# Gradients of a gated MLP: two hidden blocks per round, untransposed weight gradients, and half-filled matmuls placed side by side

## The chip, the cores and the metric

The kernel runs on one core of a Trainium2 chip. The metric is the device time of one execution in microseconds (us), as the median over several executions. Its engines are TensorE (PE; PEld is its weight load), VectorE (DVE), ScalarE (ACT), GpSimd (POOL) and SyncE (SP, which here only issues DMA). Matmuls write into PSUM, which has eight banks of 512 float32 values on each of 128 partitions; everything else lies in SBUF.

## The reference

The reference is a forward pass and its gradients. A layer normalisation with a learned shift and scale goes through a spectral filter (a 2-D FFT, a product, an inverse FFT), and a second one through a gated MLP without a nonlinearity:

```python
def _B_ref(x, w_gate, w_up, w_down):      # x: 1 x 2048 x 576, F = 4608
    g = jnp.einsum('bsd,df->bsf', x, w_gate)
    u = jnp.einsum('bsd,df->bsf', x, w_up)
    h = g * u
    return jnp.einsum('bsf,fd->bsd', h, w_down)

h = _layernorm(x) * (1 + ca) + sa
x = x + ga * _A_ref(h, A_w_r, A_w_i)
h = _layernorm(x) * (1 + cb) + sb
x = x + gb * _B_ref(h, B_w_gate, B_w_up, B_w_down)
```

The outputs are x and the gradients of eight inputs, in bfloat16. The change concerns the gated MLP alone. With 2048 tokens, 576 model dimensions and 4608 hidden units it needs, for each block of 128 hidden units:

- g and u (the projections), recomputed, and from them h = g u, gg = gh u and gu = gh g, where gh is the gradient of h (computed in an earlier stage and read back from DRAM);
- the gradients of the three weights: h^T times the incoming gradient (576 columns), and gg and gu against the normalised input;
- the contribution to the gradient of the input: gg times w_gate^T plus gu times w_up^T, summed over all 36 blocks.

576 is four and a half times 128, so wherever the model dimension lies on the partitions, a fifth piece has only 64 rows.

## The kernel before

The stage ahead of the loop computes gh for all blocks and stores it. Its staging tile `ghh_st` comes from a pool of two buffers:

```python
u4w = hs.enter_context(tc.tile_pool(name="u4w", bufs=2))
...
for j in range(nfb):
    fb = fb0 + j
    st = u4w.tile([128, NT, 128], BF, name="ghh_st")
    for sb4 in range(4):
        pt = u4ps.tile([128, 4, 128], FP32, name="u4p")
        for m in range(5):
            nc.tensor.matmul(pt[:], lhsT=wdT[:, m, j * 128:(j + 1) * 128], rhs=goT[:, 4 * sb4:4 * sb4 + 4, m, :], start=(m == 0), stop=(m == 4))
        evac(st[:, 4 * sb4:4 * sb4 + 4, :], pt[:])       # ScalarE and VectorE in turn
    nc.sync.dma_start(ghhT_d[fb * 128:(fb + 1) * 128, :], st[:].rearrange("f t p -> f (t p)"))
```

The normalised input is held twice: `h2p` with tokens on the partitions, padded from 576 to 640 columns (DP) with zeros, and `h2T`, its transpose, made by one DMA.

The loop over the 36 blocks (NFB; NT is 16 tiles of 128 tokens):

```python
gups  = tile_pool(name="gups",  bufs=3, space=PSUM)
u8ps  = tile_pool(name="u8ps",  bufs=3, space=PSUM)
u57ps = tile_pool(name="u57ps", bufs=2, space=PSUM)

def emit_u57(fb_, sfs_):                      # the three weight gradients of one block
    for ti_, (sf, rhs_n) in enumerate(((sfs_[0], gon), (sfs_[1], h2n), (sfs_[2], h2n))):
        so = stg.tile([128, DP], BF, name="so")
        for h in range(2):
            pw = u57ps.tile([128, 512], FP32, name="u57p")
            for t in range(NT):
                nc.tensor.matmul(pw[:, 0:288], lhsT=sf[:, t, :], rhs=rhs_n[:, t, h * 288:(h + 1) * 288], start=(t == 0), stop=(t == NT - 1))
            nc.scalar.copy(so[:, h * 288:(h + 1) * 288], pw[:, 0:288])
        if ti_ == 0:
            nc.sync.dma_start(out_6[...], so[:, 0:D])
        else:                                 # gate and up: to be stored transposed
            ptr = u57ps.tile([128, 5, 128], BF, name="u57p")
            for m in range(5):
                nc.tensor.transpose(ptr[0:KD[m], m, :], so[:, m * 128:m * 128 + KD[m]], ident[:])
            # ... two ScalarE copies to woT, two stores

for fb in range(NFB):
    # ... every 2nd block: load wgu, its fifth piece zeroed to 128 rows; every 4th: wT by ten DMA transposes
    for sb4 in range(4):
        ts_ = slice(4 * sb4, 4 * sb4 + 4)
        for wi_, dstT in enumerate((gT, uT)):             # the projections
            pt = gups.tile([128, 4, 128], FP32, name="gup")
            for m in range(5):
                nc.tensor.matmul(pt[:], lhsT=wgu[:, wi_, m, jw * 128:(jw + 1) * 128], rhs=h2T[:, ts_, m, :], start=(m == 0), stop=(m == 4))
            nc.scalar.copy(dstT[:, ts_, :], pt[:])
        # ... hhT = gT * uT, ggT = ghh * uT, guT = ghh * gT on VectorE
    # ... hh_sf, gg_sf, gu_sf: DMA transposes of hhT, ggT, guT; a store of hhT
    if pend:
        emit_u57(*pend.pop(0))                            # of the block before
    for t in range(NT):                                   # the gradient of the input
        for h in range(2):
            pu = u8ps.tile([128, 512], FP32, name="u8p")
            nc.tensor.matmul(pu[:, 0:288], lhsT=ggT[:, t, :], rhs=wT[:, 0, jt, h * 288:(h + 1) * 288], start=True, stop=False)
            nc.tensor.matmul(pu[:, 0:288], lhsT=guT[:, t, :], rhs=wT[:, 1, jt, h * 288:(h + 1) * 288], start=False, stop=True)
            # ... acc += pu on VectorE (a copy for the first block)
    pend.append((fb, sfs))
```

A scheduler orders the instructions of each engine, so what is written one after the other here may be mixed on the engine: before the change, the projections of a block are mixed with the input gradient of another.

Of the kernel before, what the change touches and what calls it, by code (L numbers as in the profile page):

```python
# [9 lines left out]
FP32 = mybir.dt.float32  # L10
# [9 lines left out]
NT = 16  # L20
S = 2048
D = 576
# [58 lines left out]
def build(ctx, tc, A_x, A_w_r, A_w_i, B_w_gate, B_w_up, B_w_down, c_in, w_mod, grad_out,  # L81
# [256 lines left out]
    with ExitStack() as hs:  # L338
# [62 lines left out]
        for fb0 in range(0, NFB, FB4):  # L401
# [11 lines left out]
                evac(wdT[0:64, 4, j * 128:(j + 1) * 128], ptw[0:64, 4, :])  # L413
            for j in range(nfb):
                fb = fb0 + j
                st = u4w.tile([128, NT, 128], BF, name="ghh_st")
                for sb4 in range(4):
                    pt = u4ps.tile([128, 4, 128], FP32, name="u4p")
                    for m in range(5):
                        nc.tensor.matmul(pt[:], lhsT=wdT[:, m, j * 128:(j + 1) * 128], rhs=goT[:, 4 * sb4:4 * sb4 + 4, m, :], start=(m == 0), stop=(m == 4))  # L420
                    evac(st[:, 4 * sb4:4 * sb4 + 4, :], pt[:])
                nc.sync.dma_start(ghhT_d[fb * 128:(fb + 1) * 128, :], st[:].rearrange("f t p -> f (t p)"))
# [6 lines left out]
    with ExitStack() as ms:  # L429
# [8 lines left out]
        with ExitStack() as ls:  # L438
# [5 lines left out]
            nc.vector.tensor_copy(mb2h[:], mb2[:, 0:2 * D])  # L444
            nc.gpsimd.dma_start(gon[:], go_v)
            nc.vector.tensor_tensor(out=gon[:], in0=gon[:], in1=gb_b.unsqueeze(1).to_broadcast([128, NT, D]), op=MUL)
            nc.gpsimd.memset(h2p[:, :, D:DP], 0.0)
            for c4 in range(4):
                x1c = lp2.tile([128, 4, D], FP32, name="x1c")
                nc.sync.dma_start(x1c[:], x1_d[:, 4 * c4:4 * c4 + 4, :])  # L450
# [1 line left out]
                for tt in range(4):  # L452
                    t = 4 * c4 + tt
                    n = lp2.tile([128, D], FP32, name="ln2n")
                    nc.scalar.activation(out=n[:], in_=x1c[:, tt, :], func=ACT.Identity, bias=nmr2[:, tt:tt + 1], scale=rstd2[:, tt:tt + 1])
                    nc.vector.tensor_tensor(out=n[:], in0=n[:], in1=opcb_b, op=MUL)
                    nc.vector.tensor_tensor(out=h2p[:, t, 0:D], in0=n[:], in1=sb_b, op=ADD)
            nc.sync.dma_start_transpose(out=h2T[:].rearrange("q t m p -> q (t m) p"), in_=h2p[:].rearrange("p t d -> p (t d)"))
        with ExitStack() as bs:
            FBW = 2  # L460
            FBT = 4
            wp = bs.enter_context(tc.tile_pool(name="wp", bufs=2))
            wtp = bs.enter_context(tc.tile_pool(name="wtp", bufs=2))
            ghp = bs.enter_context(tc.tile_pool(name="ghp", bufs=2))
            tp = bs.enter_context(tc.tile_pool(name="tp", bufs=2))
            tp2 = bs.enter_context(tc.tile_pool(name="tp2", bufs=2))
            sfp = bs.enter_context(tc.tile_pool(name="sfp", bufs=2))
            stg = bs.enter_context(tc.tile_pool(name="stg", bufs=4))
            wot = bs.enter_context(tc.tile_pool(name="wot", bufs=3))
            gups = bs.enter_context(tc.tile_pool(name="gups", bufs=3, space=PSUM))  # L470
            u8ps = bs.enter_context(tc.tile_pool(name="u8ps", bufs=3, space=PSUM))
            u57ps = bs.enter_context(tc.tile_pool(name="u57ps", bufs=2, space=PSUM))
            pend = []

            def emit_u57(fb_, sfs_):
                for ti_, (sf, rhs_n) in enumerate(((sfs_[0], gon), (sfs_[1], h2n), (sfs_[2], h2n))):
                    so = stg.tile([128, DP], BF, name="so")
                    for h in range(2):
                        pw = u57ps.tile([128, 512], FP32, name="u57p")
                        for t in range(NT):  # L480
                            nc.tensor.matmul(pw[:, 0:288], lhsT=sf[:, t, :], rhs=rhs_n[:, t, h * 288:(h + 1) * 288], start=(t == 0), stop=(t == NT - 1))  # L481
                        nc.scalar.copy(so[:, h * 288:(h + 1) * 288], pw[:, 0:288])  # L482
                    if ti_ == 0:
                        nc.sync.dma_start(out_6[fb_ * 128:(fb_ + 1) * 128, :], so[:, 0:D])
                    else:
                        ptr = u57ps.tile([128, 5, 128], BF, name="u57p")
                        for m in range(5):
                            K = KD[m]
                            nc.tensor.transpose(ptr[0:K, m, :], so[:, m * 128:m * 128 + K], ident[:])
                        woT = wot.tile([128, 5, 128], BF, name="woT")  # L490
                        nc.scalar.copy(woT[:, 0:4, :], ptr[:, 0:4, :])
                        nc.scalar.copy(woT[0:64, 4, :], ptr[0:64, 4, :])
                        odst = out_4 if ti_ == 1 else out_5
                        nc.sync.dma_start(odst[0:512, fb_ * 128:(fb_ + 1) * 128].rearrange("(m q) f -> q m f", q=128), woT[:, 0:4, :])
                        nc.sync.dma_start(odst[512:576, fb_ * 128:(fb_ + 1) * 128], woT[0:64, 4, :])
            wgu = None
            wT = None
            for fb in range(NFB):
                if fb % FBW == 0:
                    nb = min(FBW, NFB - fb)  # L500
                    wgu = wp.tile([128, 2, 5, FBW * 128], BF, name="wgu")
                    nc.gpsimd.memset(wgu[64:128, :, 4, :], 0.0)
                    for wi_, wsrc in enumerate((B_w_gate, B_w_up)):
                        eng = nc.sync if wi_ == 0 else nc.gpsimd
                        eng.dma_start(wgu[:, wi_, 0:4, 0:nb * 128], wsrc[0:512, fb * 128:(fb + nb) * 128].rearrange("(m q) f -> q m f", q=128))
                        eng.dma_start(wgu[0:64, wi_, 4, 0:nb * 128], wsrc[512:576, fb * 128:(fb + nb) * 128])
                if fb % FBT == 0:
                    nb = min(FBT, NFB - fb)
                    wT = wtp.tile([128, 2, FBT, D], BF, name="wT")
                    for wi_, wsrc in enumerate((B_w_gate, B_w_up)):  # L510
                        for m in range(5):
                            K = KD[m]
                            nc.sync.dma_start_transpose(out=wT[:, wi_, 0:nb, m * 128:m * 128 + K], in_=wsrc[m * 128:m * 128 + K, fb * 128:(fb + nb) * 128])
                jw = fb % FBW
                jt = fb % FBT
                ghh = ghp.tile([128, NT, 128], BF, name="ghh")
                nc.gpsimd.dma_start(ghh[:].rearrange("f t p -> f (t p)"), ghhT_d[fb * 128:(fb + 1) * 128, :])
                gT = tp2.tile([128, NT, 128], BF, name="gT")
                uT = tp2.tile([128, NT, 128], BF, name="uT")
                hhT = tp.tile([128, NT, 128], BF, name="hhT")  # L520
                ggT = tp.tile([128, NT, 128], BF, name="ggT")
                guT = tp.tile([128, NT, 128], BF, name="guT")
                for sb4 in range(4):
                    ts_ = slice(4 * sb4, 4 * sb4 + 4)
                    for wi_, dstT in enumerate((gT, uT)):
                        pt = gups.tile([128, 4, 128], FP32, name="gup")
                        for m in range(5):
                            nc.tensor.matmul(pt[:], lhsT=wgu[:, wi_, m, jw * 128:(jw + 1) * 128], rhs=h2T[:, ts_, m, :], start=(m == 0), stop=(m == 4))  # L528
                        nc.scalar.copy(dstT[:, ts_, :], pt[:])  # L529
                    nc.vector.tensor_tensor(out=hhT[:, ts_, :], in0=gT[:, ts_, :], in1=uT[:, ts_, :], op=MUL)  # L530
                    nc.vector.tensor_tensor(out=ggT[:, ts_, :], in0=ghh[:, ts_, :], in1=uT[:, ts_, :], op=MUL)
                    nc.vector.tensor_tensor(out=guT[:, ts_, :], in0=ghh[:, ts_, :], in1=gT[:, ts_, :], op=MUL)
                nc.gpsimd.dma_start(hhT_d[:, :, fb, :].rearrange("tp f x -> f tp x"), hhT[:].rearrange("f (tp ti) p -> f tp (ti p)", ti=2))  # L533
                sfs = []
                for nm, srcT in (("hh_sf", hhT), ("gg_sf", ggT), ("gu_sf", guT)):
                    sf = sfp.tile([128, NT, 128], BF, name=nm)
                    nc.sync.dma_start_transpose(out=sf[:], in_=srcT[:].rearrange("f t p -> f (t p)"))
                    sfs.append(sf)
                if pend:
                    emit_u57(*pend.pop(0))  # L540
                for t in range(NT):
                    for h in range(2):
                        pu = u8ps.tile([128, 512], FP32, name="u8p")
                        nc.tensor.matmul(pu[:, 0:288], lhsT=ggT[:, t, :], rhs=wT[:, 0, jt, h * 288:(h + 1) * 288], start=True, stop=False)  # L544
                        nc.tensor.matmul(pu[:, 0:288], lhsT=guT[:, t, :], rhs=wT[:, 1, jt, h * 288:(h + 1) * 288], start=False, stop=True)  # L545
                        dst = acc[:, t, h * 288:(h + 1) * 288]
                        if fb == 0:
                            nc.vector.tensor_copy(dst, pu[:, 0:288])
                        else:
                            nc.vector.tensor_tensor(out=dst, in0=dst, in1=pu[:, 0:288], op=ADD)  # L550
                pend.append((fb, sfs))
            emit_u57(*pend.pop(0))
        res2cm.__exit__(None, None, None)
        if "gh2" in dbg:
            nc.sync.dma_start(dbg["gh2"], acc[:])
# [279 lines left out]
```

## Time and profile before

| | |
|---|---|
| median of 4 executions | 2085.81 us |
| lowest to highest | 2081.19 to 2087.41 us |
| profiled execution | 2079.4 us |
| TensorE busy | 1661.1 us (80%) |
| VectorE busy | 1213.5 us (58%) |
| ScalarE busy | 580.7 us (28%) |

How to read the lines that follow. A group's line gives the source line, the engine, the operation, output and inputs, the shape and the count; then the busy time and the mean ns of one; then the idle time of the engine ahead of it and what ended it. A timeline line gives the start, the length (both us), the engine, and the same description; in brackets stands the idle time ahead of it. A line that begins with a stretch (434.00:1502.00) gives its length and then the busy time and instructions of PE, PEld, DVE, ACT and POOL, the granted TensorE clock as a share of full speed, the busy share of the DMA engines and GB/s. SPq is the issue of a DMA from the sync queue. In the page's slices each digit is the busy share of a fortieth of the run in tenths. Matmuls overlap each other, so the length of one says less than the distance of two starts.

### The profile page before, as it was taken

The numbers are of one execution on the slowest core, as the hardware profiler recorded it, in microseconds if no ns is written. First come the engines' busy times: TensorE is split into PE (matmuls) and PEld (weight loads), VectorE is DVE, ScalarE is ACT, GpSimd is POOL, SyncE is SP. The second block draws the span as 40 slices with busy tenths as digits, with TensorE's granted clock in tenths as the row PEclk, the third lists the DMA queues.
The fourth block names the chain that finished last, engine by engine and source line by source line (L and its number), as shares of the span: only waits on it lengthen the run. The fifth ranks groups of instructions, "written<-read, shape, count | busy, mean of one in ns | idle before, by whom it ended". The sixth has DMA issues, their size and how long they took to land. (4 is left out here: it accounts for less than half of the span.)

```text
span 2079.4 us, 30347 instructions
## 1 busy us (share of the span) xinstructions
PE 1661.1 (80%) x11495; PEld 1079.5 (52%) x11495; DVE 1213.5 (58%) x2653; ACT 580.7 (28%) x1185; POOL 318.5 (15%) x322
## 2 busy tenths in 40 slices
PE   2088988799999999999999999999857991636321
PEld 0054534356666666666666666666634771433100
DVE  1567777256556655665556555655487333388974
ACT  1254524132232322222222222223220001233233
POOL 1200001000000000000000000000102434324750
PEclk8599989899999999999999999999967995877555
DMA  7745366755765567456665766465584644071223
GB/s 275 203 141 189 134 234 177 187 132 100 153 120 118 117 131 144 97 125 130 131 128 107 143 128 124 97 125 109 153 309 167 231 142 159 18 282 58 83 95 130
DMA packets 412147, 302.82 MB, mean 146 GB/s; under 512 B 341984, under 2 KB 378848, under 8 KB 407264
## 3 DMA queue, kind: packets, MB, share of 16 engines
q1 hardware_dynamic: 390304, 208.84, 40.3%
q0 software_dynamic: 21696, 92.03, 14.7%
q8 instruction: 90, 1.47, 0.3%
q14 instruction: 57, 0.47, 0.1%
HBM read 138.63 MB, written 89.71 MB: 110 GB/s over the span
## 5 line engine op out<-in xcount | busy, mean ns | idle before, releaser
L550 DVE TENSOR_TENSOR acc<-acc,u8p 128x288 f32<-128x288 f32 x1120 | 447.0, 450 | 402.5 <-PE u8p L545 401.4
L528 PE MATMUL gup<-h2T,wgu 128*128 128x512 bf16 x1440 | 425.6, 379 | 0.7 <-ACT gT L529 0.7
L544 PE MATMUL u8p<-wT,ggT 128*128 128x288 bf16 x1152 | 315.4, 286 | 0.0
L545 PE MATMUL u8p<-wT,guT 128*128 128x288 bf16 x1152 | 315.1, 286 | 0.0
L420 PE MATMUL u4p<-goT,wdT 128*128 128x512 bf16 x720 | 179.0, 399 | 43.9 <-DVE ghh_st L137 18.7
L528 PEld LDWEIGHTS <-wgu 128*128 128x128 bf16 x1440 | 140.8, 98 | 102.0 <-issue 1.0
L482 ACT CAST so<-u57p 128x288 bf16<-128x288 f32 x216 | 86.0, 398 | 329.2 <-PE u57p L481 329.2
L616 PE MATMUL u3p<-wdr,hl 128*128 128x288 bf16 x1152 | 152.4, 295 | 12.0 <-DVE pr L626 10.1
L545 PEld LDWEIGHTS <-guT 128*128 128x128 bf16 x1152 | 112.6, 98 | 88.3
L481 PE MATMUL u57p<-gon,hh_sf 128*128 128x288 bf16 x1152 | 151.3, 286 | 0.0
L481 PE MATMUL u57p<-h2p,gu_sf 128*128 128x288 bf16 x1152 | 147.4, 286 | 0.0
L481 PE MATMUL u57p<-h2p,gg_sf 128*128 128x288 bf16 x1152 | 147.2, 286 | 0.0
L616 PEld LDWEIGHTS <-hl 128*128 128x128 bf16 x1152 | 116.0, 101 | 46.1 <-issue 13.4
L529 ACT CAST gT<-gup 128x512 bf16<-128x512 f32 x144 | 84.3, 585 | 199.1 <-PE gup L528 199.1
L420 PEld LDWEIGHTS <-wdT 128*128 128x128 bf16 x720 | 71.8, 101 | 130.3 <-issue 55.7
L529 ACT CAST uT<-gup 128x512 bf16<-128x512 f32 x144 | 84.3, 585 | 190.7 <-PE gup L528 115.5
L481 PEld LDWEIGHTS <-hh_sf 128*128 128x128 bf16 x1152 | 112.7, 98 | 34.9
L481 PEld LDWEIGHTS <-gg_sf 128*128 128x128 bf16 x1152 | 112.7, 98 | 28.4
L544 PEld LDWEIGHTS <-ggT 128*128 128x128 bf16 x1152 | 112.6, 98 | 28.4
L481 PEld LDWEIGHTS <-gu_sf 128*128 128x128 bf16 x1152 | 109.7, 98 | 29.1
L533 POOL DMA_DIRECT2D hhT_d<-hhT x36 | 33.2, 923 | 584.8 <-DVE hhT L530 497.0
L311 PE MATMUL yp<-T_IR,ut 128*128 128x288 bf16 (+1 forms) x384 | 76.8, 337 | 54.9 <-ACT gh L699 54.9
(374 smaller groups left out, 1990.3 us busy)
## 6 DMA issues: line engine op xcount, KB each, us to landing
ghhT_d<-ghh_st SPq DMA_DIRECT2D x36, 512.0 KB, 3.0
ghh<-ghhT_d POOLq DMA_DIRECT2D x36, 512.0 KB, 7.8
hhT_d<-hhT POOLq DMA_DIRECT2D x36, 512.0 KB, 6.9
hl<-hhT_d SPq DMA_DIRECT2D x8, 2304.0 KB, 9.7
out_dram<-woT SPq DMA_DIRECT2D x72, 128.0 KB, 2.2
gxc<-gx_d SPq DMA_DIRECT2D x8, 1152.0 KB, 8.4
wm<-in_w_mod_dram SPq DMA_DIRECT2D x2, 3456.0 KB, 13.9
wdn<-in_B_w_down_dram SPq DMA_DIRECT2D x9, 576.0 KB, 5.3
```

The costliest lines, as they stand in the source:

```text
L311: nc.tensor.matmul(yp[:, 0:288], lhsT=ut[0:Kf, fc, cc * 128:(cc + 1) * 128], rhs=T["IR"][0:Kf, fc, cc, h * 288:(h + 1) * 288], start=(k == ...
L420: nc.tensor.matmul(pt[:], lhsT=wdT[:, m, j * 128:(j + 1) * 128], rhs=goT[:, 4 * sb4:4 * sb4 + 4, m, :], start=(m == 0), stop=(m == 4))
L481: nc.tensor.matmul(pw[:, 0:288], lhsT=sf[:, t, :], rhs=rhs_n[:, t, h * 288:(h + 1) * 288], start=(t == 0), stop=(t == NT - 1))
L482: nc.scalar.copy(so[:, h * 288:(h + 1) * 288], pw[:, 0:288])
L528: nc.tensor.matmul(pt[:], lhsT=wgu[:, wi_, m, jw * 128:(jw + 1) * 128], rhs=h2T[:, ts_, m, :], start=(m == 0), stop=(m == 4))
L529: nc.scalar.copy(dstT[:, ts_, :], pt[:])
L533: nc.gpsimd.dma_start(hhT_d[:, :, fb, :].rearrange("tp f x -> f tp x"), hhT[:].rearrange("f (tp ti) p -> f tp (ti p)", ti=2))
L544: nc.tensor.matmul(pu[:, 0:288], lhsT=ggT[:, t, :], rhs=wT[:, 0, jt, h * 288:(h + 1) * 288], start=True, stop=False)
L545: nc.tensor.matmul(pu[:, 0:288], lhsT=guT[:, t, :], rhs=wT[:, 1, jt, h * 288:(h + 1) * 288], start=False, stop=True)
L550: nc.vector.tensor_tensor(out=dst, in0=dst, in1=pu[:, 0:288], op=ADD)
L616: nc.tensor.matmul(p2[h][:, 0:288], lhsT=hl[:, fb, ti * 128:(ti + 1) * 128], rhs=wdr[:, fb, h * 288:(h + 1) * 288], start=(fb == 0), stop= ...
```

## The change

It rewrites the loop and touches two things ahead of it. The hidden blocks are taken in groups of two (G = 2).

- The weight gradients of gate and up are computed the other way round: the normalised input is the stationary operand, so the result has the model dimension on the partitions, as the output wants it, and is not transposed afterwards. Both blocks of a group are the moving operand together (256 columns). The last 64 model dimensions of gate and up go into the two halves of one PSUM tile.
- The projections' fifth piece, with 64 rows, is no longer padded with zeros to 128. The gate's 64 rows lie on partitions 0 to 63 and the up's on 64 to 127 of one tile, and two matmuls use the upper and lower half of the array. For this the second half of the padded piece of `h2p` (and so of `h2T`) holds a copy of those 64 columns instead of zeros.
- The gradient of the input adds up both blocks in PSUM before VectorE adds it to `acc`.
- All parts of the loop share one PSUM pool of eight banks.
- `ghh_st` in the stage ahead gets four buffers instead of two.

The core of the diff (pools, names and loads cut):

```diff
-                st = u4w.tile([128, NT, 128], BF, name="ghh_st")
+                st = u4w.tile([128, NT, 128], BF, name="ghh_st", bufs=4)
...
-            nc.gpsimd.memset(h2p[:, :, D:DP], 0.0)
...
+                nc.vector.tensor_copy(h2p[:, 4 * c4:4 * c4 + 4, D:DP], h2p[:, 4 * c4:4 * c4 + 4, 512:D])
...
-            gups = bs.enter_context(tc.tile_pool(name="gups", bufs=3, space=PSUM))
-            u8ps = bs.enter_context(tc.tile_pool(name="u8ps", bufs=3, space=PSUM))
-            u57ps = bs.enter_context(tc.tile_pool(name="u57ps", bufs=2, space=PSUM))
+            gups = accps = gwps = bs.enter_context(tc.tile_pool(name="mmps", bufs=8, space=PSUM))
+            def wgrads(g0, f0, hh_sf, gg_sf, gu_sf):
+                for j in range(G):
...                  # the down projection's gradient as before: 2 x 16 matmuls of 288 columns
+                for sf, odst in ((gg_sf, out_4), (gu_sf, out_5)):
+                    wo = stg.tile([128, 4, GW], BF, name="wo")
+                    for m in range(4):
+                        pw = gwps.tile([128, G, 128], FP32, name="gwp", tag="ps")
+                        for t in range(NT):
+                            nc.tensor.matmul(pw[:], lhsT=h2p[:, t, m * 128:(m + 1) * 128], rhs=sf[:, :, t, :], start=(t == 0), stop=(t == NT - 1))
+                        nc.scalar.copy(wo[:, m, :], pw[:].rearrange("q j f -> q (j f)"))
+                    nc.sync.dma_start(odst[0:512, f0:f0 + GW].rearrange("(m q) f -> q m f", q=128), wo[:])
+                pw = gwps.tile([128, G, 128], FP32, name="gwp", tag="ps")
+                for t in range(NT):
+                    for i, sf in enumerate((gg_sf, gu_sf)):
+                        nc.tensor.matmul(pw[64 * i:64 * i + 64, :, :], lhsT=h2p[:, t, 512:576], rhs=sf[:, :, t, :], start=(t == 0), stop=(t == NT - 1))
+                nc.scalar.copy(wl[:], pw[:].rearrange("q j f -> q (j f)"))
...
+                    hhT = ghp.tile([128, NT, 128], BF, name="hhT")          # ghp: 2 buffers
+                    ggT = tp.tile([128, NT, 128], BF, name="ggT")           # tp: 3 buffers
+                    for sb8 in range(2):
+                        pss = [[gups.tile([128, 4, 128], FP32, name="gup", tag="ps") for _ in range(2)] for _ in range(2)]
+                        for pts, ts_ in zip(pss, tss):
+                            for i in range(2):
+                                r = slice(64 * i, 64 * i + 64)
+                                nc.tensor.matmul(pts[i][:], lhsT=wgu[r, 8, cs], rhs=h2T[r, ts_, 4, :], start=True, stop=False)
+                        for pts, ts_ in zip(pss, tss):
+                            for i in range(2):
+                                for m in range(4):
+                                    nc.tensor.matmul(pts[i][:], lhsT=wgu[:, 4 * i + m, cs], rhs=h2T[:, ts_, m, :], start=False, stop=(m == 3))
+                                nc.scalar.copy(dst[:], pts[i][:])
...                  # the three products on VectorE, hhT's store, the DMA transposes
+                    hh_sf[j] = sfp.tile([128, NT, 128], BF, name="hh_sf", bufs=3)
...
+                        for j in range(G):
+                            nc.tensor.matmul(pu[:, 0:288], lhsT=ggTs[j][:, t, :], rhs=wT[:, 0, j, hs_], start=(j == 0), stop=False)
+                            nc.tensor.matmul(pu[:, 0:288], lhsT=guTs[j][:, t, :], rhs=wT[:, 1, j, hs_], start=False, stop=(j == G - 1))
```

The transposed weights `wT` are loaded for two blocks at a time by ten DMA transposes, where before ten served four blocks. In the built program the instructions of TensorE in the loop are no longer mixed: each group is the projections (four full rounds of 4 half-height and 16 full matmuls), then the weight gradients of the group before, then the gradient of the input.

## The prediction

> **What bounds the kernel now.** I read the page's busy shares and its 40 slices first, then the busy time of each engine in the long middle of the run, then the costliest groups, and then the TensorE timeline of one round of that middle, because the shares alone do not say what fills a round.
>
> ```profile
> PE 1661.1 (80%) x11495; PEld 1079.5 (52%) x11495; DVE 1213.5 (58%) x2653; ACT 580.7 (28%) x1185; POOL 318.5 (15%) x322
> PE   2088988799999999999999999999857991636321
> PEclk8599989899999999999999999999967995877555
> ...
> 434.00:1502.00 1068.00, 1065.68 (x7563) 722.51 (x7561) 614.47 (x1585) 307.42 (x647) 80.64 (x119) 1.00 0.60 123
> ```
>
> From 434 to 1502 us, half of the run, TensorE (first number after the length) is busy 1065.68 of 1068 us at a granted clock of 1.00, while VectorE works 614 us and ScalarE 307. This stretch is the loop that the change rewrites, and it is TensorE's alone: only fewer TensorE cycles, or holes between them, can change its length.
>
> ```profile
> L550 DVE TENSOR_TENSOR acc<-acc,u8p 128x288 f32<-128x288 f32 x1120 | 447.0, 450 | 402.5 <-PE u8p L545 401.4
> L528 PE MATMUL gup<-h2T,wgu 128*128 128x512 bf16 x1440 | 425.6, 379 | 0.7 <-ACT gT L529 0.7
> ```
>
> The costliest group, VectorE's accumulation, is a trap: it waits 401 us for TensorE, so halving it gives nothing directly. The 379 ns of a matmul are also not its price, because matmuls overlap; what counts is the distance of their starts.
>
> ```profile
> 439.69 4.48 PE L528 MATMUL gup<-h2T,wgu 128*128 128x512 bf16 x20
> 444.01 0.29 PE L544 MATMUL u8p<-wT,ggT 128*128 128x288 bf16 x1
> ...
> 705.26 0.27 PE L489 MATMUL u57p<-ident,so 128*128 128x128 bf16 x2
> 705.37 0.29 PE L544 MATMUL u8p<-wT,ggT 128*128 128x288 bf16 x1
> 705.49 0.29 PE L545 MATMUL u8p<-wT,guT 128*128 128x288 bf16 x1
> 705.62 0.29 PE L544 MATMUL u8p<-wT,ggT 128*128 128x288 bf16 x1
> 705.91 0.46 PE L489 MATMUL u57p<-ident,so 128*128 128x128 bf16 x3
> 706.30 4.09 PE L481 MATMUL u57p<-h2p,gu_sf 128*128 128x288 bf16 x32
> 710.23 0.28 PE L489 MATMUL u57p<-ident,so 128*128 128x128 bf16 x2
> ```
>
> Twenty 512-column matmuls take 444.01 - 439.69 = 4.32 us, 0.216 each. Thirty-two of 288 columns take 710.23 - 706.30 = 3.93 us, 0.1228 each. The five transposes of a gradient block, from 705.26 to 706.30, take 1.04 us with three 288-column matmuls inside (0.37), so they cost 0.67 us, not the 0.28 that five back to back would (a run of 73 in the chain of waits takes 4.26 us, 0.058 each): the second half waits for ScalarE's copy of "so". One block of the loop is then 40 x 0.216 + 64 x 0.1228 + 96 x 0.1228 + 2 x 0.67 = 8.64 + 7.86 + 11.79 + 1.34 = 29.63 us; 36 blocks make 1067, as the stretch says. The account closes, so I use it for the kernel after.
>
> The one other place that the change touches is the end of the stage before:
>
> ```profile
> 349.43 19.08 SPq L458 DMA_TRANSPOSE h2T<-h2p  x1
> 354.65 4.49 PE L420 MATMUL u4p<-goT,wdT 128*128 128x512 bf16 x20
> 368.60 1.00 SPq L422 DMA_DIRECT2D ghhT_d<-ghh_st  x2
> 372.46 14.98 PE L420 MATMUL u4p<-goT,wdT 128*128 128x512 bf16 x60 [13.33 <-ACT ghh_st L135]
> ...
> 360.00:434.00 74.00, 55.06 (x258) 24.80 (x258) 19.32 (x32) 15.14 (x31) 0.52 (x1) 0.88 0.63 175
> ```
>
> The stores of ghh_st stand behind a 19 us transpose in the sync queue, both staging buffers are full, and TensorE stands still for 13.3 us; in all it is idle 74 - 55 = 19 us there.
>
> **What the Trainium skill says.** "TensorE: Matmul & The Clock Gate", section "Back-to-back issue gap", gives N/2.4 + 2.5 ns for a warm matmul of N columns: 215.8 and 122.5 ns for 512 and 288. The trace agrees (216 and 122.8). The page's Part 3 on row and column tiling says that matmuls in different row or column groups of the array run at the same time, with 2.38x for three column tiles; "TensorEngine Tiling (Array Packing)", section "Key Properties", adds that a change of the tiling mode drains TensorE, and its section "Restrictions" that column tiling switches the fast weight load off. No matmul of this trace is tiled in pairs, so none of these three is shown here yet.
>
> **The change part by part**, per group of two blocks, 59.26 us before.
>
> (1) The transposes of the two gate and up gradients go, four sets of 0.67: -2.68 us. The gradient now comes out with the model dimension on the partitions, so it needs none.
>
> (2) Gate and up gradients: before, 128 matmuls of 288 columns, 128 x 0.1228 = 15.72 us. After, 128 of 256 columns plus 32 of 256 columns that use only half the array's columns (the last 64 rows of the output). From the two measured distances a column costs (0.216 - 0.1228)/224 = 0.416 ns, so 256 columns cost 0.1095 us: 128 x 0.1095 = 14.02. The 32 narrow ones are 3.50 us one after the other and 1.75 in perfect pairs. The half-width weight load is not cheaper in this trace (106 ns against 98 in the by-shape view of the transposes' loads), so I estimate 0.14 a pair, 2.24, and 0.1 for each of two mode changes. Sum 16.46, that is +0.74.
>
> (3) Gate and up projections: before 80 x 0.216 = 17.28. After, 64 full ones (13.82) and 16 of half height, the last 64 of 576 input rows, in two row groups: 3.46 serial, 1.73 in perfect pairs; I estimate 0.25 a pair, 2.0. They stand as four in front of every 16 full ones (the order of the built program shows just this), so there are eight mode changes a group, at an estimated 0.1 each, 0.8. Sum 16.62: -0.66.
>
> (4) The input gradient stays at 128 x 0.1228 = 15.72, the down-projection gradient at 64 x 0.1228. What changes is that two blocks add up in PSUM: VectorE's accumulations halve from 1152 to 576, some 576 x 0.45 = 259 us of VectorE work, and ScalarE loses 144 transposed copies. All lies beside TensorE and is worth nothing by itself. It does let the stage run without mixing: VectorE adds at 11.54/29 = 0.40 us (29 in a row in its timeline), and an output now comes every 4 x 0.1228 = 0.49 us instead of every 0.25.
>
> Sum: -2.68 + 0.74 - 0.66 = -2.60 a group, x 18 = -47 us.
>
> (5) Four staging buffers for ghh_st: two more blocks of 4.3 us of matmuls can run while the queue is blocked, and the small waits after it (1.5, 1.1 and 4.0 us in the timeline) mostly go. Of 19 us I give 15: -15 us.
>
> (6) The first group: its input gradient follows its projections at once, with one copy and three products to wait for, +3 us. The memset and copy of 64 columns that make the second half of the padded tile are below 1 us and not on TensorE.
>
> Total 2085.8 - 47 - 15 + 3 = 2027 us.
>
> **The rivals.** A, the halves don't overlap, or the mode change eats what they save. Then (2) is +1.8 with no mode cost, (3) is +0.8 with it, and with -2.68 the loop gains almost nothing; only -15 + 3 remain: about 2072. For it: no tiled pair in the trace, a short run of four between drains, and a weight load of 106 ns that is no shorter for half the columns. Against it: row and column groups differ in the built program, the pairs write different banks or different partitions, and they are adjacent.
>
> B, everything overlaps and mode changes are free: (2) +0.05, (3) -1.73, sum -4.36 a group, -78, with 18 from the head about 1992.
>
> C, a new wait appears: the matmuls of the loop are no longer mixed, so any late buffer leaves a hole. The candidates are the sync queue (ten half-size weight transposes a group instead of five for each two, at 1.26 us each, plus six large ones at 1.8 to 8 us: about 43 of 57 us), hh_sf with three buffers, and PSUM, which all parts now share in turn. From the order and the buffers each has some 30 us of slack before TensorE needs it; the banks come round after eight outputs, against copies of 0.4 to 0.6 us. A hole of 1 us a group would cost 18 us, so C could bring 2045 to 2060; I give it little.
>
> D, VectorE was the true limit. The window shows TensorE 99.8% busy, so no.
>
> **Range and chances.** Between A (2072) and B (1992) the centre is 2027; the two mode costs and the pairing move it by 30 us either way. I say 1996 to 2058 for 8 in 10. Faster by over 2% means under 2044: 0.76. Within 2%: 0.22, mostly A or C. Slower by over 2% needs a large new wait: 0.02.
>
> **What would show it.** The loop should take about 1020 us instead of 1068, with TensorE still near 99%. The half-height four should start as two close pairs, some 0.5 us together; if they start 0.216 apart, A holds. Thirty-two narrow ones should take 2.2 us; 3.5 means no overlap. The idle before the first full matmul after a change is the mode cost; over 0.2 us and (3) becomes a loss. Idle before the u4p matmuls between 340 us and the loop should fall from 19 to about 4 us. VectorE's accumulation should be 576 instructions with the loop no shorter for it. Idle of TensorE on hh_sf, wT or ghh, or a slower clock, would prove C.

## The result, and the profile after

| | before | after |
|---|---|---|
| median | 2084.64 us (13 executions) | 2009.36 us (8 executions) |
| lowest to highest | 2081.19 to 2087.41 us | 2007.11 to 2013.78 us |
| TensorE busy in the loop | 1065.4 of 1067.8 us | 1005.3 of 1005.6 us |
| VectorE busy in the loop | 614 us | 432 us |
| ScalarE busy in the loop | 307 us | 257 us |

The changed kernel takes 0.9642 of the time before (95% interval 0.9633 to 0.9652): 75 us less. The profiled execution of the changed kernel took 2017.6 us (its trace spans 2015.8), 8 above the median, and that of before 2081.2 us (2079.4), 3 below its own; so where an execution's head is concerned (everything ahead of the loop), I compare medians of kernels rather than two profiles.

Busy shares and slices of the page of the changed kernel, and its loop in the windows view (after the length: busy time and instructions of PE, PEld, DVE, ACT, POOL, then the granted clock, DMA share, GB/s):

```profile
PE 1599.2 (79%) x11711; PEld 1064.4 (53%) x11711; DVE 1032.9 (51%) x2081; ACT 531.1 (26%) x1059; POOL 304.6 (15%) x303
PE   2078979889999999999999999999657973727221
PEclk8589989999999999999999999999778985867555
```

```profile
431.39:1437.00 1005.61, 1005.32 (x7776) 707.18 (x7775) 431.54 (x1008) 257.32 (x522) 71.89 (x102) 1.00 0.62 129
```

The loop is still TensorE's alone: 0.3 us of 1005.6 idle, at a clock of 1.00. It is 62 us shorter, and the page's PE sum fell by the same 62 us (1661.1 to 1599.2). What follows the loop is unchanged: 2079.4 - 1502.3 = 577 us before, 2015.8 - 1437.0 = 579 us after. So of the 75 us about 62 are the loop and, by subtraction, 13 the head.

The TensorE timeline of the first group's projections in the changed kernel (start, length, engine, description):

```profile
431.39 0.61 PE L525 MATMUL gup<-h2T,wgu 64*128 64x512 bf16 x4 [0.67 <-ACT ghh_st L135]
431.94 3.63 PE L530 MATMUL gup<-h2T,wgu 128*128 128x512 bf16 x16
435.49 0.60 PE L525 MATMUL gup<-h2T,wgu 64*128 64x512 bf16 x4
...
443.69 0.60 PE L525 MATMUL gup<-h2T,wgu 64*128 64x512 bf16 x4
444.23 3.63 PE L530 MATMUL gup<-h2T,wgu 128*128 128x512 bf16 x16
447.69 0.29 PE L552 MATMUL accp<-wT,ggT 128*128 128x288 bf16 x1
```

Read the starts: a round takes 435.49 - 431.39 = 4.10 us. Four half-height matmuls take 431.94 - 431.39 = 0.55 us, sixteen full ones 3.55. Twenty full ones took 4.32 before. If each of the two pairs costs as much as one full matmul, a round is 18 x 0.216 = 3.89; the 0.21 left over are the two mode changes, 0.105 each. Note also the last line: the first group's input gradient follows its projections without a gap.

The weight gradients of a middle group, same view:

```profile
703.17 8.00 PE L475 MATMUL gwp<-gon,hh_sf 128*128 128x288 bf16 x64
711.01 7.15 PE L483 MATMUL gwp<-gg_sf,h2p 128*128 128x256 bf16 x64
717.99 7.15 PE L483 MATMUL gwp<-gu_sf,h2p 128*128 128x256 bf16 x64
725.07 0.30 PE L490 MATMUL gwp<-gg_sf,h2p 128*64 128x256 bf16 x1
725.08 0.30 PE L490 MATMUL gwp<-gu_sf,h2p 128*64 128x256 bf16 x1
725.21 0.27 PE L490 MATMUL gwp<-gg_sf,h2p 128*64 128x256 bf16 x1
725.21 0.27 PE L490 MATMUL gwp<-gu_sf,h2p 128*64 128x256 bf16 x1
...
726.74 0.27 PE L490 MATMUL gwp<-gg_sf,h2p 128*64 128x256 bf16 x1
726.94 0.30 PE L552 MATMUL accp<-wT,ggT 128*128 128x288 bf16 x1
```

The 128 full ones take 725.07 - 711.01 = 14.06 us. Of the narrow ones, gate and up start together, within 0.01 us, and from the second pair on they follow each other by (726.74 - 725.21) / 14 = 0.109 us, which is the price of one matmul of 256 columns: the pairs overlap fully. All 32 take 726.94 - 725.07 = 1.87 us. From the last pair to the next full-width matmul it is 0.20 us, so the change back to full width costs about 0.09.

The group that led the page before, VectorE's accumulation, in the changed kernel:

```profile
L558 DVE TENSOR_TENSOR acc<-acc,accp 128x288 f32<-128x288 f32 x544 | 246.8, 454 | 407.7 <-PE accp L553 388.6
```

Half as many, and still 389 us of waiting for TensorE.

### The profile page after: what moved, and what is told of

It is laid out like the page before. It is cut to its first block, busy times and chain, and to the rows that moved or that the text cites. A ratio compares the mean times of both kernels' runs of the same rounds, so it can differ in the third digit from the quotient of the medians.

```text
span 2015.8 us, 29571 instructions
## 1 busy us (share of the span) xinstructions
PE 1599.2 (79%) x11711; PEld 1064.4 (53%) x11711; DVE 1032.9 (51%) x2081; ACT 531.1 (26%) x1059; POOL 304.6 (15%) x303
## 5 line engine op out<-in xcount | busy, mean ns | idle before, releaser
L558 DVE TENSOR_TENSOR acc<-acc,accp 128x288 f32<-128x288 f32 x544 | 246.8, 454 | 407.7 <-PE accp L553 388.6
L552 PE MATMUL accp<-wT,ggT 128*128 128x288 bf16 x1152 | 283.1, 286 | 0.0
L553 PE MATMUL accp<-wT,guT 128*128 128x288 bf16 x1152 | 283.0, 286 | 0.0
L530 PE MATMUL gup<-h2T,wgu 128*128 128x512 bf16 x1152 | 261.1, 380 | 0.0
L483 PEld LDWEIGHTS <-h2p 128*128 128x128 bf16 x2304 | 225.4, 98 | 26.6
L475 PE MATMUL gwp<-gon,hh_sf 128*128 128x288 bf16 x1152 | 144.1, 286 | 0.0
L483 PE MATMUL gwp<-gu_sf,h2p 128*128 128x256 bf16 x1152 | 128.7, 273 | 0.0
L483 PE MATMUL gwp<-gg_sf,h2p 128*128 128x256 bf16 x1152 | 128.7, 273 | 0.0
L536 DVE TENSOR_TENSOR guT<-ghh,gT 128x512 bf16<-128x512 bf16 x144 | 61.2, 425 | 74.0 <-ACT gT L532 69.7
L534 DVE TENSOR_TENSOR hhT<-gT,uT 128x512 bf16<-128x512 bf16 x144 | 61.2, 425 | 68.8 <-ACT uT L532 68.8
```

What stands on the lines that cost most here:

```text
L475: nc.tensor.matmul(pw[:, 0:288], lhsT=hh_sf[j][:, t, :], rhs=gon[:, t, h * 288:(h + 1) * 288], start=(t == 0), stop=(t == NT - 1))
L483: nc.tensor.matmul(pw[:], lhsT=h2p[:, t, m * 128:(m + 1) * 128], rhs=sf[:, :, t, :], start=(t == 0), stop=(t == NT - 1))
L530: nc.tensor.matmul(pts[i][:], lhsT=wgu[:, 4 * i + m, cs], rhs=h2T[:, ts_, m, :], start=False, stop=(m == 3))
L534: nc.vector.tensor_tensor(out=hhT[:, ts_, :], in0=gu[0][:], in1=gu[1][:], op=MUL)
L552: nc.tensor.matmul(pu[:, 0:288], lhsT=ggTs[j][:, t, :], rhs=wT[:, 0, j, hs_], start=(j == 0), stop=False)
L553: nc.tensor.matmul(pu[:, 0:288], lhsT=guTs[j][:, t, :], rhs=wT[:, 1, j, hs_], start=False, stop=(j == G - 1))
```

## The experiments

Eleven kernels were run. "us" is the median. Every one is compared with the kernel before on the same chip, and the ratios are to it.

### Undoing or doing one part of the loop

**The transposes alone.** The kernel before, without the ten transposes and the two copies to woT per block; the two gradients are stored as they come out, so their layout is left out.

```diff
-                        for m in range(5):
-                            nc.tensor.transpose(ptr[0:K, m, :], so[:, m * 128:m * 128 + K], ident[:])
-                        # ... the two copies to woT
+                        # stores straight from so
```

> The kernel before without the ten transposes of a block and without the two ScalarE copies of their results; the untransposed gradients are stored in their place with stores of nearly the same sizes, so the layout of two outputs is left out. Theory 1 (a set of five transposes costs 0.67 us of TensorE, as read in the timeline): 72 x 0.67 = 48 us less than before, about 2037 us. Theory 2 (only the back-to-back price of the transposes, 360 x 0.058 = 21 us, because other matmuls fill the wait): about 2064 us.

Measured: 2036.07 us, ratio 0.9762 [0.9743, 0.978], 50 us less. This term is what the prediction's 0.67 us per gradient block says, 18 x 2.68 = 48. It is by far the largest of the change.

**The narrow ones in turn.** The changed kernel with the sixteen narrow gate matmuls ahead of the sixteen up ones, so that program-order neighbours use the same half of the columns.

```diff
-                for t in range(NT):
-                    for i, sf in enumerate((gg_sf, gu_sf)):
+                for i, sf in enumerate((gg_sf, gu_sf)):
+                    for t in range(NT):
```

> The changed kernel with the order of the 32 half-width matmuls of a group changed: first the 16 of the gate, then the 16 of the up weights, so that neighbours use the same half of the array's columns. Theory 1 (the two column halves ran at the same time and each pair cost one matmul of 0.109 us): 16 x 0.109 = 1.75 us more per group, 18 groups, 31 us more than the changed kernel, about 2041 us. Theory 2 (the trace only draws them side by side and the array took them in turn): no difference, 2009 us.

Measured: 2034.72 us, ratio 0.9769 [0.9749, 0.979], 25 us more than the changed kernel; the loop, from its first matmul to the end of its last, is 1029.4 us against 1005.3, 24 longer. So the pairs are worth 24 us, and rival A is out for this part. It falls a little short of the expected 31, and the timeline of this run says why:

```profile
491.57 1.61 PE L490 MATMUL gwp<-gg_sf,h2p 128*64 128x256 bf16 x13
492.91 0.30 PE L490 MATMUL gwp<-gu_sf,h2p 128*64 128x256 bf16 x1
493.01 0.27 PE L490 MATMUL gwp<-gg_sf,h2p 128*64 128x256 bf16 x1
493.04 0.27 PE L490 MATMUL gwp<-gu_sf,h2p 128*64 128x256 bf16 x1
493.12 0.27 PE L490 MATMUL gwp<-gg_sf,h2p 128*64 128x256 bf16 x1
493.15 0.27 PE L490 MATMUL gwp<-gu_sf,h2p 128*64 128x256 bf16 x1
493.23 0.27 PE L490 MATMUL gwp<-gg_sf,h2p 128*64 128x256 bf16 x1
493.26 1.58 PE L490 MATMUL gwp<-gu_sf,h2p 128*64 128x256 bf16 x13
494.77 0.30 PE L552 MATMUL accp<-wT,ggT 128*128 128x288 bf16 x1
```

At the seam three up matmuls start before the last gate ones, which stand ahead of them in the program: the records show the other half of the columns being used up to three matmuls early. Three of sixteen are thus paired even here, and the 32 take 494.77 - 491.57 = 3.20 us instead of the 3.50 of one after the other.

**The fifth piece at full height.** The changed kernel with the four half-height matmuls reaching over all 128 rows; gate and up each then get the sum of both fifth pieces, so their separation is left out. This removes both the pairs and the mode changes of the projections.

```diff
-  nc.tensor.matmul(pts[i][:], lhsT=wgu[r, 8, cs], rhs=h2T[r, ts_, 4, :], ...)
+  nc.tensor.matmul(pts[i][:], lhsT=wgu[:, 8, cs], rhs=h2T[:, ts_, 4, :], ...)
```

> The changed kernel with the projections' fifth piece as full-height matmuls: each uses all 128 rows of the tile that holds the gate's 64 rows and the up's 64 rows, so both projections get the sum of the two fifth pieces and the separation is left out; the count of instructions is the same. Theory 1 (a row pair costs one matmul, and the two mode changes of a round cost about 0.2 us together): a round goes from 4.10 to 20 x 0.216 = 4.32 us, 72 rounds, 16 us more than the changed kernel, about 2025 us. Theory 2 (mode changes cost as much as the pairs save): no difference, 2009 us.

Measured: 2028.17 us, ratio 0.9736 [0.972, 0.9753]; the loop is 1021.3 us, 15.9 longer than the changed kernel's. The row pairs pay 16 us net of their mode changes.

**Half the mode changes.** The changed kernel, with every second round doing its half-height matmuls last, so that those of two rounds stand together: four mode changes a group in place of eight.

```diff
-                        # 4 half-height, then 16 full, in each of the two rounds of a block
+                        # round 0: 16 full, then 4 half-height; round 1: 4 half-height, then 16 full
```

> The changed kernel with the half-height matmuls of every second round put after its full ones, so that the fours of two rounds stand together: 16 full, 8 half-height, 32 full, 8 half-height, 16 full for a group, four mode changes instead of eight. Theory 1 (of the 4.10 us of a round 0.21 are its two mode changes): four changes of 0.105 us less per group, 18 groups, 7.6 us less than the changed kernel, about 2002 us. Theory 2 (the 0.21 us belong to each pair, not to the change): no difference. A rival for the worse: two rounds now end in the same moment and need all eight banks, so the copies out of PSUM leave holes of about 1 us a group, 18 us more.

Measured: 2006.1 us, ratio 0.9611 [0.9596, 0.9626]; the loop 997.9 us, 7.5 shorter. That is 7.5 us for 18 x 4 = 72 changes, 0.104 each, in agreement with the 0.105 read above. The median is only 3 us under the changed kernel's (6 by the two ratios); the loop is the better measure, since kernels that differ only in the loop start it between 421 and 431 us in their profiles. Its timeline:

```profile
427.43 3.61 PE L530 MATMUL gup<-h2T,wgu 128*128 128x512 bf16 x16 [0.67 <-ACT ghh_st L135]
430.98 1.04 PE L526 MATMUL gup<-h2T,wgu 64*128 64x512 bf16 x8
431.95 7.08 PE L530 MATMUL gup<-h2T,wgu 128*128 128x512 bf16 x32
```

Eight half-height ones take 431.95 - 430.98 = 0.97 us: four pairs of 0.216 and one change.

**An addition for each block.** The changed kernel with VectorE's accumulation of every single block, as before (1152 instructions instead of 576); TensorE has the same matmuls to do, though the scheduler placed some of them differently.

```diff
-  pu = accps.tile(...)                      # one PSUM tile for the G blocks
-  for j in range(G): # two matmuls each, start at j == 0, stop at j == G - 1
-  # one add to acc
+  for j in range(G):
+      pu = accps.tile(...)                  # one for each block
+      # two matmuls, one add to acc
```

> The changed kernel with the gradient of the input taken out of PSUM after each block, as before the change: 1152 additions of VectorE instead of 576, all else the same, and the loop stays unmixed. Theory 1 (adding two blocks up in PSUM is what lets the unmixed loop run): an output comes every 2 x 0.123 = 0.245 us and VectorE adds one in 0.40, so 64 outputs take 25.6 instead of 15.7 us; less what eight banks buffer (some 2 us), about 8 us a group, 18 groups, 140 us more, about 2150 us. Theory 2 (VectorE's saving was idle time and is worth nothing): 2009 us.

Measured: 2133.17 us, ratio 1.0229 [1.0209, 1.0249], 124 us more than the changed kernel and slower than the kernel before. Its loop in the windows view, its accumulation as the costliest group, and pieces of its VectorE and TensorE timelines:

```profile
426.60:1555.10 1128.50, 1128.03 (x7776) 707.57 (x7775) 594.28 (x1584) 257.12 (x521) 71.89 (x102) 1.00 0.56 115
```

```profile
L558 DVE TENSOR_TENSOR acc<-acc,accp 128x288 f32<-128x288 f32 x1120 | 414.4, 448 | 386.5 <-PE accp L554 384.4
```

```profile
698.63 6.64 DVE L558 TENSOR_TENSOR acc<-acc,accp 128x288 f32<-128x288 f32 x18
```

```profile
701.32 0.28 PE L553 MATMUL accp<-wT,ggT 128*128 128x288 bf16 x1
701.44 0.28 PE L554 MATMUL accp<-wT,guT 128*128 128x288 bf16 x1
701.68 0.28 PE L553 MATMUL accp<-wT,ggT 128*128 128x288 bf16 x1
701.81 0.28 PE L554 MATMUL accp<-wT,guT 128*128 128x288 bf16 x1
```

This is the profile to be wary of. The window calls TensorE busy for 1128.03 of 1128.5 us, and the group says that VectorE waits for TensorE; yet VectorE sets the pace. The starts betray it: 0.12 us inside a pair, but 0.36 from one output to the next (0.364 as the mean of 28, from 699.86 to 710.07 in the same view) where two matmuls need 0.25. VectorE's additions come at the same pace: 18 of them, each 0.45 us long and begun before the last one ends, take 6.64 us. The eight banks are full and each output waits for an addition to free one. That wait does not appear as idle time, because the recorded length of a matmul, 0.28 us, reaches over the 0.24 us to the next start.

Of the 64 outputs of a group the first 15 still come every 0.245 us; in all they take 715.90 - 694.33 = 21.57 us instead of 15.72. Over 18 groups that is 105 of the 123 us that the loop is longer. The other 18 come from the order of this build: in the first round of projections behind the outputs, half-height and full matmuls now alternate.

```profile
715.90 0.37 PE L525 MATMUL gup<-h2T,wgu 64*128 64x512 bf16 x1
716.21 0.39 PE L530 MATMUL gup<-h2T,wgu 128*128 128x512 bf16 x1
716.53 0.39 PE L525 MATMUL gup<-h2T,wgu 64*128 64x512 bf16 x1
...
721.05 0.61 PE L525 MATMUL gup<-h2T,wgu 64*128 64x512 bf16 x4
```

Its two pairs are lost and six mode changes are added, so this round takes 721.05 - 715.90 = 5.15 us instead of 4.10, in 17 of the 18 groups. The addition in PSUM is thus worth about 105 us here, still more than the 75 that the whole change gained.

### The stage ahead of the loop

**Two staging buffers in the changed kernel**, and **four in the kernel before**:

```diff
-                st = u4w.tile([128, NT, 128], BF, name="ghh_st", bufs=4)
+                st = u4w.tile([128, NT, 128], BF, name="ghh_st")
```

> The changed kernel with two staging buffers for ghh_st again; nothing else differs. The changed kernel's profile shows 3 us less before the loop than the old one, where the prediction had 15. Theory 1 (the staging buffers did pay about 10 to 15 us, and the one profiled run of the changed kernel hid it behind other differences of the start): 2020 to 2025 us. Theory 2 (they pay only the 3 us that the two profiles show): 2010 to 2014 us.

> The kernel before with four staging buffers for ghh_st, nothing else. Theory 1: 10 to 15 us less than before, 2070 to 2075 us. Theory 2: at most 4 us less, 2080 to 2085 us.

Measured: two buffers in the changed kernel, 2030.03 us, ratio 0.9743 [0.9724, 0.9762], 21 us more than with four. Four in the kernel before, 2066.62 us, ratio 0.9913 [0.9898, 0.9928], 18 us less, with its loop at 1067.7 us as ever. So the buffers pay 18 to 21 us, more than the 15 predicted. But with two buffers the changed kernel's loop is 1005.3 us, 62.4 less than before, and its total only 54.6 us less: something else in the change makes the head about 8 us longer. The sync queue (SPq) of the changed kernel with two buffers:

```profile
341.51 8.95 SPq L422 DMA_DIRECT2D ghhT_d<-ghh_st  x3
351.53 0.38 SPq L500 DMA_DIRECT2D wgu<-in_B_w_gate_dram  x1
352.26 24.37 SPq L458 DMA_TRANSPOSE h2T<-h2p  x1
```

One store of ghh_st more and the load of wgu now stand ahead of the h2p transpose, and it takes 24 us instead of 19.

**The padding alone.** The kernel before with the copy of 64 columns by VectorE in place of GpSimd's memset, which gives the same shift in the queue.

```diff
-            nc.gpsimd.memset(h2p[:, :, D:DP], 0.0)
+                nc.vector.tensor_copy(h2p[:, 4 * c4:4 * c4 + 4, D:DP], h2p[:, 4 * c4:4 * c4 + 4, 512:D])
```

> The kernel before, two staging buffers, with one part of the change: the padding of h2p is a copy by VectorE in each of the four quarters instead of one memset by GpSimd (the other factor's rows stay zero, so the products are the same). It puts one more ghh_st store and the load of wgu ahead of the h2p transpose in the sync queue, as in the changed kernel with two buffers. Theory 1 (this shift of the queue is what made the stage ahead of the loop some 9 us longer): the transpose takes 24 us instead of 19, the loop starts near 443 instead of 434.5 us, total about 2094 us. Rival (the loads of the new loop, earlier and of another size, did it): start at 434 to 436, total about 2085 us.

Measured: 2090.39 us (20 executions), ratio 1.0028 [1.0019, 1.0037]: 5 us more than the kernel before, between the two theories. Its transpose, and TensorE's wait for it:

```profile
348.86 0.38 SPq L505 DMA_DIRECT2D wgu<-in_B_w_gate_dram  x1
349.60 23.18 SPq L458 DMA_TRANSPOSE h2T<-h2p  x1
```

```profile
375.06 2.29 PE L528 MATMUL gup<-h2T,wgu 128*128 128x512 bf16 x5 [13.27 <-DMA h2T<-h2p]
```

The longer transpose comes with the copy alone, and with the copy come 5 of the 8 us. The path between the two is not isolated: the build also moved five projections into the stage ahead, where they wait 13.3 us for the transpose itself, while the changed kernel with two buffers waits 16.2 us for a staging buffer. Why the transpose lasts longer stays open. The additional store alone is not enough: the kernel before with four buffers has the same three stores in front of its transpose and not the load of wgu, and the transpose takes 19.5 us. Whether the other 2 or 3 us come from the new loop's loads stays open too.

**The stores from ScalarE's queue.** The changed kernel with the ghh_st stores issued by ScalarE, so as not to stand behind the transposes.

```diff
-                nc.sync.dma_start(ghhT_d[...], st[...])
+                nc.scalar.dma_start(ghhT_d[...], st[...])
```

> The changed kernel with the stores of ghh_st issued from ScalarE's queue instead of the sync queue, so that they no longer stand behind the 23 us transpose of the normalised input and the ten weight transposes. Theory 1 (order in the sync queue is what holds TensorE in the end of the stage ahead): the 13 us of idle TensorE between 360 us and the loop mostly go, about 1998 us. Theory 2 (the transposes keep the DMA engines themselves busy, and a store issued earlier lands no earlier): no difference, 2009 us.

Measured: 2034.07 us, ratio 0.9751 [0.9727, 0.9776]: 25 us worse than the changed kernel, which neither theory allowed for. Sync queue, ScalarE and TensorE of this run:

```profile
352.62 34.24 SPq L458 DMA_TRANSPOSE h2T<-h2p  x1
```

```profile
392.91 1.07 ACT L135 CAST ghh_st<-u4p 128x512 bf16<-128x512 f32 x2 [28.42 <-DMA wT<-in_B_w_gate_dram]
408.13 1.07 ACT L135 CAST ghh_st<-u4p 128x512 bf16<-128x512 f32 x2 [14.15 <-DMA wT<-in_B_w_gate_dram]
```

```profile
393.55 7.42 PE L420 MATMUL u4p<-goT,wdT 128*128 128x512 bf16 x20 [24.28 <-ACT ghh_st L135]
408.77 5.56 PE L420 MATMUL u4p<-goT,wdT 128*128 128x512 bf16 x15 [7.81 <-ACT ghh_st L135]
```

The other queue did not let the stores pass. ScalarE stands still for 28 and 14 us and is released by the landing of a weight transpose that belongs to the sync queue, and TensorE stands behind ScalarE's copies. In the built program the DMAs of both queues take eight completion semaphores in turn, and ahead of such a store ScalarE waits for the semaphore that a weight transpose of the sync queue had before it. That fits the releaser in the trace; a run without the shared semaphores was not made.

**The transpose in four.** The changed kernel with the h2p transpose issued for each quarter of the tokens as soon as it is ready.

```diff
+                nc.sync.dma_start_transpose(out=h2T[:, 4 * c4:4 * c4 + 4]..., in_=h2p[:, 4 * c4:4 * c4 + 4]...)
-            nc.sync.dma_start_transpose(out=h2T[:]..., in_=h2p[:]...)
```

> The changed kernel, with the one transpose of h2p (23.3 us in the sync queue) issued as four, one for each quarter of the tokens as it is ready. Theory 1 (the one long transpose is what holds the stores of ghh_st and so TensorE): four pieces of about 6 us let the stores pass between them, the idle of TensorE between 350 us and the loop (about 12 us in the changed kernel) mostly goes, the loop starts near 420 instead of 431 us, and the whole takes about 2000 us. Rival (the stores wait for the DMA engines, busy either way, and each piece adds a fixed cost): no gain or up to 8 us lost, 2009 to 2017 us. The loop itself stays at 1006 us under both.

Measured: 2005.04 us, ratio 0.9626 [0.9608, 0.9644], 4 us less than the changed kernel, with overlapping intervals. The pieces stand 3 to 7 us in the queue each, and in its profile the loop starts at 417 us. Against the changed kernel's profile that would be 14 us, but most of it is the difference between two executions: the changed kernel's variants with the same head start their loops between 421 and 431 us. A small gain, below the 10 expected.

**Both together**, the split transpose and half the mode changes:

> The split transpose and the halved number of mode changes together, on the changed kernel. If both gains add (mode changes -7.7 us in the loop, the split -10 us ahead of it) 1990 to 1996 us; if the split gains nothing, 2003 to 2008 us.

Measured: 1997.33 us (1994.52 to 2001.49), ratio 0.9585 [0.9566, 0.9603]. The best version: 12 us under the changed kernel, 9 under the one with the mode changes alone. The intervals of that second step just overlap as well: both steps lean to a small gain from the split, and neither shows it clear of noise.

## Why the prediction was right

It said 2027 us, from 1996 to 2058, and faster; measured were 2009. The sum of its six terms was -59 us, and -75 came. By terms:

| term | predicted | measured | from |
|---|---|---|---|
| (1) transposes gone | -48 | -50 | the run without them |
| (2) gate and up gradients | +13 | +4 | 14.06 + 1.87 = 15.93 against 15.72 us, x 18 |
| (3) projections | -12 | -16 | 4 x 4.10 = 16.40 against 17.28 us, x 18; -16 by the full-height run |
| (4) fewer additions | 0 | 0 as placed | but +105 in the loop without it (+123 with the order of that build) |
| (5) staging buffers | -15 | -18 to -21 | two runs |
| (6) first group | +3 | 0 | no gap at 447.69 |
| not foreseen: the head | 0 | +8, of which +5 with the padding copy | two runs |

The table adds up to between -72 and -75.

**(1)** held in count and price, but the reason given for the price covers less than half of it. A set costs 0.67 us where five transposes back to back would take 0.28. The wait for ScalarE's copy ahead of the third one is 705.91 - 705.62 = 0.29 us where a matmul of 288 columns takes 0.12, so it makes 0.17 of the 0.39 us between the two. The larger part is the fifth transpose, which has only 64 columns:

```profile
705.98 0.39 PE L489 MATMUL u57p<-ident,so 128*128 128x128 bf16 x2
```

```profile
706.13 0.24 PE L489 MATMUL u57p<-ident,so 128*64 128x128 bf16 x1
706.30 0.30 PE L481 MATMUL u57p<-h2p,gu_sf 128*128 128x288 bf16 x1
```

The first line's two are the fourth and the fifth. The fifth starts 0.15 us after the fourth, and the next matmul 0.17 after it, where transposes in a row are 0.06 apart: 0.21 us for the change to half width and back. So the kernel before paid for mode changes as well, some 72 x 0.21 = 15 us, and its trace held the price that the prediction guessed at 0.1. With the change these are gone too.

**(2)** was mis-sized, by 0.53 us a group, nearly all of it on the pair. The estimate of 0.14 us a pair allowed for a weight load that does not keep up; 0.109 was measured, as if the second matmul were free. The mode change, guessed at 0.1, was about 0.09. "TensorEngine Tiling (Array Packing)", section "Restrictions", of the Trainium skill says that column tiling does without the fast weight load; here that costs nothing that can be seen in the distance of pairs, 0.109 us. What "TensorE: Matmul & The Clock Gate" says in its Part 3 on packing small matmuls, that tiles in different column groups run at the same time, holds in full: 1.87 us against 3.20 with the two halves in turn.

**(3)** was mis-sized by 0.22 us a group, again on the pair: 0.216 instead of 0.25. The mode change, guessed at 0.1, was 0.105.

**(4)** was right about this change, and its reason was half right. The prediction said that the halved additions are worth nothing by themselves, because they lie beside TensorE. It also said that they let the stage run without mixing, and that is the part that counts. In the kernel before, an addition every 0.25 us would have been too much for VectorE as well, which needs 0.36 in a row; there the scheduler spread the outputs among projections and weight gradients. The new order puts all of them in one stretch, and without the addition in PSUM the change would have lost some 105 us and come out slower. That it is "worth nothing" can hold for the old order only, and there it rests on VectorE's 401 us of waiting: no run halves the additions in that order.

**(5)** was too small as a term, and the net of the head (-13, by subtraction) close to the predicted -15 only because the new kernel's head lost some 8 us elsewhere, 5 of them with the copy for the padding, which the prediction set below 1 us. That is a right sum from two errors, and so luck. Its sign did not come: between 340 us and the loop TensorE is idle 91.39 - 78.34 = 13 us in the changed kernel's profile, and 4 were forecast.

**(6)** fell: the products were ready in time.

Of the rivals, A is refuted by the starts in the timeline and by the two runs that undo the pairs (24 and 16 us more in the loop). C is refuted by the account: at the prices of the shapes (0.216, 0.1228 and 0.109 us a matmul or a pair, about 0.1 a mode change) the stages take 16.4 + 7.9 + 15.9 + 15.7 = 55.9 us a group, and 18 groups make 1006 us, the whole loop, which leaves no room for a hidden wait. B had the pairs right and the mode changes wrong: these still cost 18 x 8 x 0.105 = 15 us in the projections, half of which the reordered version got back. (Its parts add up to 1990 us, not 1992.) D was rightly dismissed for before and after, but not for the reason given: the run with an addition for each block is limited by VectorE at a busy share of 99.96% of TensorE. What excludes D in the kernel before is that the distances of starts without any wait for VectorE already make its 1067 us.

## What to carry to other kernels

Where a tuned loop is all matmuls, price it by the distance of starts, shape by shape; once that account closes for the kernel before, it prices what has the same shapes in the rewrite; here the loop lost 62 us where 47 were forecast, and the difference lies mostly in the pairs, which that trace did not hold. Here a remainder that fills half the array paid in pairs of adjacent instructions, and more so with the pairs gathered in fewer places. Before outputs are put back to back, check that the engine which empties PSUM can take them at that rate: if it can't, TensorE looks busy while it waits.

## What was not expected of the hardware

- Narrow matmuls in the other half of the columns start up to three places ahead of program order. "TensorE: Matmul & The Clock Gate", section "Step-by-step: what each phase is for", says that matmuls stay in program order and only weight loads are pulled ahead; the records of the run with the halves in turn (492.91 before 493.01, 493.12 and 493.23) show otherwise, and the total of 3.20 us instead of 3.50 fits them.
- A change between full and half-height matmuls costs 0.105 us (0.104 by the run with half of them), and one between full and half width about as much (0.21 us for both ways in the kernel before, 0.09 for the way back in the changed one).
- With the stores on ScalarE's queue, ScalarE stood still for 28 us until a transfer of the sync queue landed, and its copies with it.
- The same transpose of h2p took 19 us in one order of the queue and 23 to 24 in another, and 34 with the stores on a second queue.
